# Loading one chunk of q later in a sliding-window attention and gated feed-forward kernel

## The chip, the cores and the metric

The kernel runs on one core of a Trainium2 chip. The metric is the device time of one execution in microseconds (us); the time of a version is the median of several executions. A profiled execution of the version before is used for everything that is said of its inside.

The engines of a core work side by side: PE multiplies matrices, DVE and ACT do elementwise work, POOL does elementwise work and also issues loads, SP issues stores and transposes. Sixteen DMA engines move the data; the loads that POOL issues go through one queue (q0 in the profile), SP's transfers through another (q1).

## The reference

Eight batches with eight heads, 576 tokens and 64 elements per head. Each token attends to itself and the 63 tokens before it; the result goes through a feed-forward layer with the gate h * cos(h).

```python
scores = scale * np.matmul(q, k.transpose(0, 1, 3, 2))      # q, k, v: (8, 8, 576, 64)
rel = pos[:, None] - pos[None, :]
mask = (rel >= 0) & (rel < 64)
scores = np.where(mask, scores, -1000000000.0)
attn = softmax(scores)
x = np.matmul(attn, v)                                      # to (4608, 512)
h = x @ w_in                                                # w_in: (512, 2048)
out = (h * np.cos(h)) @ w_out                               # w_out: (2048, 512)
```

## The kernel before

The 4608 tokens are cut into nine tiles of 512. For each tile `mt` from 1 on, PE runs through the same stage: 64 matmuls for `h_ps` (L512), with the sine on ACT (L748) and the gate on DVE (L751), and then 64 for `out_ps` (L764; from tile 6 on a form with fewer products, L601). Between them, attention work for later tiles is put in: in tile `mt` the scores of batch `mt + 1` (L327, two bursts: the first after the `h_ps` matmuls, the second after 24 of the `out_ps` matmuls), then mask and row maximum on DVE (L380), exponentials on ACT (L392), reciprocals on DVE (L402), normalised weights `w` on POOL (L409), and their transposition to `wT` by DMA from SP (L428). At the end of tile `mt` PE forms the value products of tile `mt + 1` (L444: 64 small matmuls of `wT` and `v`), copies take them to `xT`, and the next tile's `h_ps` starts from there. So the value products stand between two stages, and they need the last `wT` that the tile made. A tile's weights come in five groups (tile 2) or four (tiles 3 to 5) before this point, and more after it, whose `wT` are read one tile later.

q and k of a batch from 2 on are loaded in five chunks of up to 128 tokens, all heads at once: four chunks of 128 rows and a fifth of 64 (`load_chunk`, issued by POOL at L186, with the conversion to bf16). They are turned by DMA transposes that SP issues (`turn`, L243), three for q into `qT` and three for k into `kT`: chunks 0 and 1, chunks 2 and 3, chunk 4 (`TURNS`, L45). v is loaded in five chunks as well (L192), and POOL copies halves of it to shifted places (`spread_v`, L130).

What stands where is set by a plan: `at(time, function, arguments)` (L615) puts a step at a planned time, and `pump` (L618) emits all steps up to a time, in the order of their times. A tile is 32 units of this plan. Each engine then works through its own instructions in that order, and an instruction that waits for data holds up everything behind it on its engine. Planned times are an order only; the chip doesn't know them. The loop at L648 plans the loads of the batches from 2 on. For batch 4, `t0` is 96 and the loads fall into tile 2 (times 64 and on): its q chunks are at 5.6 + 1.6 c behind 64 (L655), of its k chunks the first two in between, and chunks 2 to 4 at 24.2 + 0.01 c (L657). `spread_v` of batch 3 is at 24.0 and 24.1 in the same count (L670), the three turns of q of batch 4 at 24.3, 24.32 and 24.34 (L651), the turns of k six units ahead of tile 3 and in the order of L662.

Of the kernel before, what the change touches and what calls it, by code (L numbers as in the profile page):

```python
# [43 lines left out]
NB = 5  # L44
# [30 lines left out]
def kernel(  # L75
# [539 lines left out]
    def at(time, fn, *args):  # L615
        plan.append((time, len(plan), fn, args))
# [8 lines left out]
    for i, (b, jobs, banks) in enumerate(bursts):  # L625
        t = T * (b - 1)
        at(t + (BURST[i % 2] + 0.9 * (i == 1) if b < B - 1 else (17.2, T + 14.6)[i % 2]), burst_scores, i)
        for n in range(jobs[0][0], jobs[-1][-1] + 1):
            place = (n - n_listed) % NU
            time = t + BURST[0] + PACE * place  # L630
# [17 lines left out]
    for b in range(2, B):  # L648
        t0 = T * (b - 1)
        for lo, hi in TURNS:  # L650
            at(t0 - (2.01 - 0.1 * lo if b == 2 else T - (24.3 if b == 4 else 23.4) - 0.01 * lo), turn_q, b, lo, hi)  # L651
        if b > 2:
            for c in range(NB):
                for i, name in enumerate(("q", "k")):
                    time = 17.9 + 2.8 * i if b == 3 and c == NB - 1 else 5.6 + 1.6 * c + 0.8 * i  # L655
                    if name == "k" and (b == 3 or c > (1 if b == 4 else 2)):
                        time = ((24.31 if c > 1 else 13) if b == 3 else 24.2 if b == 4 else 22.4) + 0.01 * c  # L657
                    if b > 4 and c == 0:
                        time = (24.26 if b == 5 else 22.46) + 0.01 * i - T
                    at(t0 - T + time, load_chunk, name, b, c)  # L660
        for lo, hi in TURNS:
            at(t0 + 0.1 * lo - (2 if b == 2 else 6), turn_k, b, lo, hi)  # L662
        for c in range(5):
            at(t0 + (10.1 + 0.1 * c if b == B - 1 else 0.5 + c), load_v, b, c)
        for half_ in range(2):
            if b == 2:
                at(t0 + 24.1 + 0.01 * half_, spread_v, b, half_, "p", 0, 2)
                at(t0 + 24.2 + 0.1 * half_, spread_v, b, half_, "p", 2, 4)
            else:
                at(t0 + (24 if b == 3 else 27.5 if b == B - 1 else 22.2) + 0.1 * half_, spread_v, b, half_)  # L670
    for mt in range(2, n_mt):
        for p in range(PAIRS):
            time = T * mt - 1.01
# [130 lines left out]
```

## Time and profile before

| what | value |
| --- | --- |
| three runs | 296.73, 297.04, 298.02 us; median 297.04 |
| the profiled execution | 296.9 us |
| its span, from the first to the last instruction | 295.1 us |
| granted TensorE clock | 1.000 |
| stage of tile 2 in the trace | 87.3 to 118.4 us |
| stage of tile 3 in the trace | 118.4 to 148.8 us |
| q0, the queue of POOL's loads | 100896 packets, 18.06 MB |
| q1, SP's queue | 67184 packets, 25.15 MB |

The page gives each engine's busy time over the span, the chain of work that ended last, and groups of instructions. Times in its rows are us from the span's start. A group that ends with a bracket was idle before it, and the bracket names what ended that. A DMA row gives the KB and the us from issue to landing.

### The profile page before, as it was taken

What the parts mean: (1) busy time and instruction counts of PE and PEld (TensorE: products, weight loads), DVE (VectorE), ACT (ScalarE), POOL (GpSimd) and SP (SyncE); (2) the same over time, 40 slices, a digit from 0 to 9 for tenths busy, and PEclk for the clock granted to TensorE, in tenths of its full rate; (3) what the DMA queues carried; (4) which work ended last, traced back from release to release, by engine and by line L of the source; (5) the groups of instructions that cost most, each with busy time, mean ns of one, the idle gap of its engine ahead of it and who ended that gap; (6) DMA issues with size and microseconds to landing.
All of it is one profiled execution on the core that took longest, in us unless ns stands there. A gap on an engine that the chain in (4) does not pass through costs nothing.

```text
span 295.1 us, 8290 instructions
## 1 busy us (share of the span) xinstructions
PE 287.7 (97%) x2815; PEld 162.7 (55%) x2815; DVE 230.6 (78%) x906; ACT 238.1 (81%) x791; POOL 210.0 (71%) x230
## 2 busy tenths in 40 slices
PE   8979999999999999999999999999999999999995
PEld 3658854544454444444454545444547854884595
DVE  4988888887897876788678876996689878957853
ACT  5998699888987799879987999799977896937710
POOL 9899659992899659994999399948995476133200
PEclk9999999999999999999999999999999999999999
DMA  7999999999999999999999999999959415042013
GB/s 139 180 199 205 192 193 146 150 136 149 186 214 137 144 227 153 143 178 216 171 171 144 220 168 161 147 211 187 144 121 192 53 38 178 2 116 84 0 38 107
DMA packets 168267, 43.81 MB, mean 148 GB/s; under 512 B 155616, under 2 KB 163872, under 8 KB 168224
## 3 DMA queue, kind: packets, MB, share of 16 engines
q0 software_dynamic: 100896, 18.06, 84.0%
q1 hardware_dynamic: 67184, 25.15, 48.0%
q8 instruction: 22, 0.36, 0.5%
q14 instruction: 21, 0.17, 0.2%
q10 hardware_dynamic: 144, 0.07, 0.1%
HBM read 36.70 MB, written 9.44 MB: 156 GB/s over the span
## 4 chain that ended last, share of the span: by engine, by line
PE 85%; POOL 6%; DMA 3%; ACT 3%; DVE 1%; issue 1%; POOLq 0%
PE h_ps L512 37%; PE out_ps L764 19%; PE out_ps L601 13%; PE h_ps L476 5%; PE o_ps L444 3%; PE out_ps L495 3%; ACT e L392 2%; PE s_ps L327 2%; POOL w L409 2%; DMA k<-in_k_dram 2%; DMA wT<-w 1%; POOL v L192 1%; PE tw_ps L425 1%; POOL w_in L208 1%; POOL v L130 1%
## 5 line engine op out<-in xcount | busy, mean ns | idle before, releaser
L512 PE MATMUL h_ps<-xT,w_in 128*128 128x512 bf16 x512 | 111.8, 379 | 0.0
L409 POOL TENSOR_TENSOR w<-e,rden 128x512 bf16<-128x512 f32 (+1 forms) x68 | 69.5, 1033 | 47.9 <-DVE rden L402 36.7
L751 DVE TENSOR_TENSOR gT<-h_ps,sin 128x512 bf16<-128x512 f32 x128 | 84.6, 687 | 21.8 <-ACT sin L748 20.4
L392 ACT ACTIVATE e<-s,negm 128x128 f32<-128x128 f32 (+1 forms) x256 | 97.2, 382 | 2.6 <-DVE negm L380 1.6
L748 ACT ACTIVATE sin<-h_ps 128x512 f32<-128x512 f32 x128 | 73.6, 599 | 25.4 <-PE h_ps L512 23.5
L512 PEld LDWEIGHTS <-w_in 128*128 128x128 bf16 x512 | 50.0, 98 | 59.5
L764 PE MATMUL out_ps<-w_out,gT 128*128 128x512 bf16 x320 | 72.0, 380 | 0.0
L380 DVE CUSTOM_DVE_ANT_0 s<-s_ps,mask 128x128 f32<-128x128 f32 (+1 forms) x256 | 55.8, 277 | 0.3 <-PE s_ps L327 0.3
L764 PEld LDWEIGHTS <-gT 128*128 128x128 bf16 x320 | 30.4, 98 | 35.4
L392 ACT ACTIVATION_READ_ACCUMULATOR e<-s,negm 128x1 f32 x256 | 48.1, 188 | 0.0
L192 POOL DMA_DIRECT2D v<-in_v_dram x40 | 34.0, 874 | 0.4 <-issue 0.3
L186 POOL DMA_DIRECT2D q<-in_q_dram x30 | 26.3, 888 | 4.0 <-PE tq_ps L225 2.8
L186 POOL DMA_DIRECT2D k<-in_k_dram x30 | 26.2, 884 | 0.0
L402 DVE RECIPROCAL rden<-den 128x4 f32<-128x4 f32 (+1 forms) x73 | 12.0, 167 | 17.8 <-ACT e L392 17.6
L130 POOL COPY v<-v 64x1536 bf16<-64x1536 bf16 (+3 forms) x16 | 22.9, 1431 | 0.4
L380 DVE DVE_READ_ACCUMULATOR2_ANT negm<- 128x1 f32 x256 | 21.3, 83 | 0.0
L541 POOL TENSOR_TENSOR qT<-gT 128x512 bf16<-128x512 bf16 x12 | 13.6, 1151 | 9.1 <-DVE gT L751 9.0
L130 DVE CAST xT<-o_ps 128x512 bf16<-128x512 f32 x24 | 15.5, 681 | 5.7 <-PE o_ps L444 5.5
L601 PEld LDWEIGHTS <-gT 128*128 128x128 bf16 x152 | 14.0, 98 | 2.2
L495 PE MATMUL out_ps<-w_out,gT 128*128 128x512 bf16 x64 | 14.7, 380 | 0.0
L476 PE MATMUL h_ps<-xT,w_in 128*128 128x256 bf16 x128 | 14.6, 273 | 0.0
L572 DVE TENSOR_TENSOR out_sb<-out_ps,p 128x512 f32<-128x512 f32 (+2 forms) x16 | 8.6, 549 | 6.7 <-ACT p L130 5.6
(92 smaller groups left out, 326.0 us busy)
## 6 DMA issues: line engine op xcount, KB each, us to landing
out_dram<-out_sb SPq DMA_DIRECT2D x16, 512.0 KB, 8.8
v<-in_v_dram POOLq DMA_DIRECT2D x32, 128.0 KB, 6.0
q<-in_q_dram POOLq DMA_DIRECT2D x24, 128.0 KB, 9.0
k<-in_k_dram POOLq DMA_DIRECT2D x24, 128.0 KB, 6.7
w_in<-in_moe_w_in_dram POOLq DMA_DIRECT2D x4, 512.0 KB, 9.3
w_out<-in_moe_w_out_dram POOLq DMA_DIRECT2D x4, 512.0 KB, 10.7
q<-in_q_dram POOLq DMA_DIRECT2D x7, 144.0 KB, 5.8
k<-in_k_dram POOLq DMA_DIRECT2D x7, 144.0 KB, 5.9
```

What stands on the lines that cost most here:

```text
L130: {"a": nc.scalar.copy, "p": nc.gpsimd.tensor_copy}.get(engine, nc.vector.tensor_copy)(out, in_)
L186: nc.gpsimd.dma_start(out=st[name, b][0:n, c].rearrange("p (h d) -> p h d", h=H), in_=src.rearrange("h p d -> p h d"))
L192: nc.gpsimd.dma_start(out=vt.rearrange("p (h d) -> p h d", h=H), in_=v[b, :, c * 128:c * 128 + n, :].rearrange("h p d -> p h d"))
L380: nc.vector.tensor_tensor_reduce(out=s[:, u, c], in0=s_ps[:, u, c], in1=mask[:, 2 - j % 2 if j else 0, c], scale=-scale if b else -1.0, sc ...
L392: nc.scalar.activation(e[:, u, c], s[:, u, c], AF.Exp, bias=negm[:, u:u + 1], scale=1.0 if n < n_first else -1.0, accum_out=den[:, u:u + 1])
L409: (nc.gpsimd if engine == "p" else nc.vector).tensor_tensor(out=w[:, 0:u], in0=e[:, 0:u], op=ALU.mult, in1=rden[:, 0:u].unsqueeze(2).to_br ...
L476: nc.tensor.matmul(out=h_ps[:, half * e:half * e + half], lhsT=w_in_sb[:, ks, ff * 128:ff * 128 + 128], rhs=st["xT", 0][:, ks, half * g:ha ...
L512: nc.tensor.matmul(out=st["h", ff], lhsT=w_in_sb[:, ks, ff * 128:ff * 128 + 128], rhs=st["xT", mt][:, ks], start=start, stop=stop)
L601: nc.tensor.matmul(out=to[n_] if split else to[:, e], lhsT=lhs[name][f // 2][:, f % 2, 128 * e:128 * e + 128], rhs=rhs[name][:, f, lo:hi], ...
L748: nc.scalar.activation(sin, h_ps, AF.Sin, bias=math.pi / 2.0)
L751: nc.vector.tensor_tensor(out=gt[:, e], in0=h_ps, in1=sin, op=ALU.mult)
L764: nc.tensor.matmul(out=o_ps[e], lhsT=gT[ff // 2][:, ff % 2, ms * 128:ms * 128 + 128], rhs=w_out_sb[:, ff], start=ff == 0, stop=ff == n_ff - 1)
```

## The change

Of batch 4, the load of q's fifth chunk (64 rows) is planned at 24.19 instead of 12.0, in the count in which k's chunks 2 to 4 stand at 24.22 to 24.24. No other step's time is changed.

```diff
@@ -655,6 +655,8 @@
                     time = 17.9 + 2.8 * i if b == 3 and c == NB - 1 else 5.6 + 1.6 * c + 0.8 * i
                     if name == "k" and (b == 3 or c > (1 if b == 4 else 2)):
                         time = ((24.31 if c > 1 else 13) if b == 3 else 24.2 if b == 4 else 22.4) + 0.01 * c
+                    if name == "q" and b == 4 and c == NB - 1:
+                        time = 24.19
                     if b > 4 and c == 0:
                         time = (24.26 if b == 5 else 22.46) + 0.01 * i - T
                     at(t0 - T + time, load_chunk, name, b, c)
```

On POOL, in the middle of tile 2, the load moves behind five weight products (`w`) and two copies of v, to the place ahead of k's chunks 2 to 4. The names in brackets are the counters that an instruction waits for: DMASW those of POOL's own earlier loads, DMAHW those of SP's transfers, DVE and Pool those of the engines.

```order
 L186 DMA q<-in_q_dram 128x8x64 [waits DMASW2_49]
 L186 DMA q<-in_q_dram 128x8x64 [waits DMASW3_49]
-L186 DMA q<-in_q_dram 64x8x64 [waits DMASW4_49]
 L409 TENSOR_TENSOR w<-e,rden 128x512 [waits DMAHW6_49,DVE_49]
 L409 TENSOR_TENSOR w<-e,rden 128x512 [waits DMAHW7_49,DVE_49]
 L409 TENSOR_TENSOR w<-e,rden 128x512 [waits DMAHW0_49,DVE_49]
 L409 TENSOR_TENSOR w<-e,rden 128x512 [waits DVE_49] x2
-L130 COPY v_78<-v_78 64x3x512
+L130 COPY v_78<-v_78 64x3x512 [waits DMASW4_49]
 L130 COPY v_78<-v_78 64x4x512 [waits Pool_49]
+L186 DMA q<-in_q_dram 64x8x64
 L186 DMA k<-in_k_dram 128x8x64 [waits DMASW5_49]
```

Only the 64-row load moved; the wait for an earlier load (DMASW4, one of v's) that it had carried is now carried by the first copy. As no other load stands between the two places, the loads follow each other in the same order as before.

On SP no row moved. At the end of tile 2 stand there, in both kernels, the last transpose of w that tile 3's value products read, the three turns of q, one more transpose of w and the three turns of k:

```order
L428 DMA_TRANSPOSE wT<-w 128x4x128 [waits DMAHW0_49,Pool_49]
L243 DMA_TRANSPOSE qT_75<-q 128x8x128 [waits DMASW6_49,DMAHW1_49,DMASW0_49,PE_49]
L243 DMA_TRANSPOSE qT_75<-q 128x8x128 [waits DMASW3_49,DMAHW2_49,DMASW2_49,PE_49]
L243 DMA_TRANSPOSE qT_75<-q 128x4x64 [waits DMAHW3_49,DMASW4_49,PE_49]
L428 DMA_TRANSPOSE wT<-w 128x4x128 [waits DMAHW4_49,Pool_49]
L243 DMA_TRANSPOSE kT<-k 128x8x128 [waits DMAHW5_49,DMASW7_49,DMASW1_49]
L243 DMA_TRANSPOSE kT<-k 128x8x128 [waits DMAHW6_49,DMASW6_49,DMASW5_49]
L243 DMA_TRANSPOSE kT<-k 128x4x64 [waits DMAHW7_49,DMASW7_49]
```

The third turn of q (64 columns wide) is the one that waits for the moved load (its DMASW4); in the program it stood behind the load by five weight products and two copies of POOL, and now nothing of POOL's stands between the two.

## The prediction

> **What bounds the kernel now.** I read the head of the page first, then the chain that ended last in order of time, then the busy time by stage.
>
> ```profile
> span 295.1 us, 8290 instructions
> PE 287.7 (97%) x2815; PEld 162.7 (55%) x2815; DVE 230.6 (78%) x906; ACT 238.1 (81%) x791; POOL 210.0 (71%) x230
> ```
>
> PE is busy for 287.7 of 295.1 us. A change in loads can only win what PE waits, and the whole kernel holds 7.4 us of that, the start and the end included. So the question is small: does PE wait anywhere for something that the moved load delays, and does the move make it wait elsewhere? I call the moved load (q, batch 4, fifth chunk, 64 rows) the tail. The next rows are the chain where it leaves PE near the tail, and the stage of tile 2 beside that of tile 3 (columns: stage, its length, busy us of PE, PEld, DVE, ACT, POOL with counts, clock, DMA share, GB/s).
>
> ```profile
> 111.01 1.04 POOL w L409
> 112.05 0.55 POOL v L130
> 112.60 4.42 DMA wT<-w
> 87.30:118.40 31.10, 30.77 (x265) 14.67 (x264) 23.15 (x109) 27.20 (x95) 25.06 (x27) 1.00 1.74 164
> 118.40:148.80 30.40, 30.40 (x265) 14.49 (x264) 23.23 (x109) 27.19 (x95) 25.73 (x28) 1.00 1.91 177
> ```
>
> With the same 265 matmuls tile 2 takes 31.10 us and tile 3 takes 30.40: 0.70 us more. The chain says where: the last normalised weights (w, POOL, 111.01 to 112.05) go through one DMA transpose, issued at 112.60 and landed 4.42 us later, at 117.02. PE's timeline shows who reads it (start, us, what, idle before); the last row is the view of PE's waits from 56 to 240 us, which holds no other (us in total, times, longest).
>
> ```profile
> 116.15 0.62 PE L444 MATMUL o_ps<-wT,v 128*64 128x64 bf16 x14
> 117.07 0.98 PE L444 MATMUL o_ps<-wT,v 128*64 128x64 bf16 x50 [0.30 <-DMA wT<-w]
> 147.24 1.20 PE L444 MATMUL o_ps<-wT,v 128*64 128x64 bf16 x64
> ...
> PE o_ps L444 <- DMA wT<-w: 0.3, 1, 0.3
> ```
>
> The 64 value products of a tile take 1.20 us undisturbed (tile 3). Here 14 start at 116.15, the fifteenth needs that last transpose, and the 64 end at 117.07 + 0.98 = 118.05: 1.90 us. So 1.90 - 1.20 = **0.70 us is all that PE loses here**, the same as the difference of the stages (the view of waits counts only the 0.3 between the two groups, since a matmul's modelled end lies later than the start of the next).
>
> **The change, step by step.** One instruction moves on POOL. These are POOL's rows around its old and its new place.
>
> ```profile
> 101.21 0.69 POOL L186 DMA_DIRECT2D q<-in_q_dram  x1 [0.95 <-DMA kT<-k]
> 104.97 1.03 POOL L409 TENSOR_TENSOR w<-e,rden 128x512 bf16<-128x512 f32 x1 [3.07 <-DVE rden L402]
> 112.00 3.41 POOL L130 COPY v<-v 64x1536 bf16<-64x1536 bf16 x2
> 115.35 2.50 POOL L186 DMA_DIRECT2D k<-in_k_dram  x3
> 119.66 4.03 POOL L409 TENSOR_TENSOR w<-e,rden 128x512 bf16<-128x512 f32 x4
> 131.31 1.65 POOL L186 DMA_DIRECT2D q<-in_q_dram  x2
> 136.06 1.03 POOL L409 TENSOR_TENSOR w<-e,rden 128x512 bf16<-128x512 f32 x1 [3.10 <-DVE rden L402]
> ```
>
> 1. At the old place POOL gets 0.69 us back, and the 0.95 us that it waited there. Worth nothing: its next work waits 3.07 us for DVE anyway.
>
> 2. At the new place, 115.35, everything behind on POOL starts 0.69 us later: three k chunks, two first chunks of batch 5, four w, v's loads, batch 5's chunks. The last of these would end at 131.31 + 1.65 + 0.69 = 133.65, and at 136.06 POOL waits 3.10 us for DVE: the delay is gone there. The four w are read by tile 4 at 147 and cover it.
>
> 3. The gain: the tail's packets leave the software queue (q0), which shares the 16 DMA engines with the transposes (q1). Landings first (the last figure is us from issue): the tail, tile 2's last transpose of w, tile 5's (with its issue at 202.48), and a lone one after 240 us. Then the packets, MB and share of q0 from 112 to 114, 114 to 116 and 120 to 122 us.
>
> ```profile
> q<-in_q_dram POOLq DMA_DIRECT2D x1, 64.0 KB, 13.7
> wT<-w SPq DMA_TRANSPOSE x1, 4.4
> 202.48 1.19 SPq L428 DMA_TRANSPOSE wT<-w  x1
> wT<-w SPq DMA_TRANSPOSE x1, 3.6
> wT<-w SPq DMA_TRANSPOSE x1, 2.4
> q0 software_dynamic: 414, 0.05, 40.0%
> q0 software_dynamic: 21, 0.00, 2.0%
> q0 software_dynamic: 1489, 0.19, 354.7%
> ```
>
> The tail landed at 101.21 + 13.7 = 114.9, so it was in the engines during the last transposes of w. Its 64 KB are 512 packets of 128 B (0.19 MB in 1489 packets is 128 B each). When q0 had most of the engines it moved 1489 packets in 2 us; 512 packets are then 0.69 us of all engines. How much of that the last transpose sees is not in the trace. **Lower end 0**: from 114 to 116 q0 moved only 21 packets, so most of its backlog had left before the transpose (4.4 us) had much in flight, and a lone transpose takes 2.4 us of the 4.4 whatever is taken away. **Upper end 0.70**, all that PE waits: q0's last packets still came after 114, just when the tail landed, and the slowest engine sets the landing; the last transpose of tile 5's w took 3.6, 0.8 us less than this one. Could it come later instead? In this stretch only work is taken out, so I exclude it. I take **0.5 us**, nearer to the 0.69 of engine time than to zero, because the landing 114.9 lies inside this transpose's flight of 112.6 to 117.0.
>
> 4. The new wait: SP turns q in three transposes, and the third reads the tail. SP works in order, so what stands behind waits too: one transpose of w, the three of k, three of w, two stores. SP's rows, then the landings of the three k transposes, then the first k load at 115.35 and the last, then the two places at which PE reads k and q of batch 4.
>
> ```profile
> 117.16 1.46 SPq L243 DMA_TRANSPOSE qT<-q  x1
> 120.72 1.51 SPq L428 DMA_TRANSPOSE wT<-w  x1
> 122.33 1.25 SPq L243 DMA_TRANSPOSE kT<-k  x1
> 126.19 1.20 SPq L243 DMA_TRANSPOSE kT<-k  x1
> kT<-k SPq DMA_TRANSPOSE x1, 4.4
> kT<-k SPq DMA_TRANSPOSE x1, 6.5
> k<-in_k_dram POOLq DMA_DIRECT2D x1, 128.0 KB, 5.0
> k<-in_k_dram POOLq DMA_DIRECT2D x1, 64.0 KB, 6.9
> 132.12 0.59 PE L327 MATMUL s_ps<-kT,qT 64*64 64x64 bf16 x32
> 137.92 0.86 PE L327 MATMUL s_ps<-kT,qT 64*64 64x128 bf16 x40
> ```
>
> A load issued at 115.35 behind the same copies landed in 5.0 us with twice the bytes, so I put the tail at 115.35 + 5.0 = 120.35. The third turn of q starts there instead of at 117.16, 3.2 us later, and ends at 121.81; the transpose of w (its w ready at 119.66 + 1.03 + 0.69 = 121.38) then runs to some 123.4, and k's first turn starts near 123.5 instead of 122.33: **1.2 us late**, because 2.1 us of the hold fall into time in which SP was waiting for POOL's w. It lands at 123.5 + 4.4 = 127.9; PE wants it at 132.12. Cover left: 4.2 us. k's last turn waits for the last k load (now some 1.4 us later at most: 0.69 for its issue, as much for the tail's packets), starts near 127.6 and lands at 134.1, and PE reads it only late in the burst at 137.92: 3.8 us left. Cost **0** for PE, while that cover lasts.
>
> 5. Given back in tile 3: batch 5's loads are 0.69 us later against the transposes of w there, and PE comes 0.5 us sooner. The row of the last such transpose and its landing:
>
> ```profile
> 141.63 1.19 SPq L428 DMA_TRANSPOSE wT<-w  x1
> wT<-w SPq DMA_TRANSPOSE x1, 4.8
> ```
>
> It landed at 141.63 + 4.8 = 146.43, 0.81 us ahead of PE's products at 147.24. If the whole shift of 0.69 + 0.5 = 1.19 us came through, PE would wait 0.38 us; if w's transposes simply follow PE, nothing. I take nothing, since the w there follow DVE (3.10 us of wait at 136.06), which follows PE; 0.4 stays as the upper end.
>
> The sum: 0 (POOL) - 0.5 (stall of tile 2) + 0 (SP's hold) + 0 (tile 3) = -0.5 us. The profiled execution took 296.9 us, with a span of 295.1; 296.9 - 0.5 = 296.4. The median of the runs before, 297.04, lies 0.14 above the profiled execution, so by the median it would be 296.5, which I predict.
>
> A rule bears on step 3. The Trainium skill, "DMA: Bandwidth & Descriptors", section "Queues, rings and completion order", says that each DMA engine takes turns between the queues it has work for, a packet at a time. By that rule every packet of the tail taken away gives the transposes its turn, and the gain would be the full stall; the row with 21 packets of q0 speaks against so much. That is the third rival below.
>
> **Rivals.**
>
> *No gain (chance 0.28).* The last transpose is slow by its own issue and completion, not by the tail. For: 2.4 us of 4.4 stay in any case, and q0 had 21 packets left after 114. Against: the tail's landing at 114.9. Or the gain is won and given back in tile 3. Then 296.9, up to 297.3 with step 5's 0.4.
>
> *SP held too long (0.07): slower.* These rows are the medians of the 64 KB loads of q and of k.
>
> ```profile
> q<-in_q_dram POOLq DMA_DIRECT2D x6, 64.0 KB, 12.6
> k<-in_k_dram POOLq DMA_DIRECT2D x6, 64.0 KB, 5.8
> ```
>
> If the tail still took its 13.7 us, it would land at 129.05; the turn ends at 130.5, the transpose of w at 132.1, k's first turn lands at 132.2 + 4.4 = 136.6, and PE, which wants it at 132.12, stands still for 4.5 us: 301.4. It decides from a landing of 9.2 us on (k's first turn must start by 127.72; 1.46 + 1.51 and two gaps of 0.1 before it). For: q's median of 12.6. Against: those loads stood last behind the others; k's, issued where the tail now goes, take 5.8. The Trainium skill speaks for still less: the same page, section "Anatomy of one DMA", fits a DMA from GpSimd by about 2.0 us and its bytes over 436 GB/s, an estimate of 2.15 us for 64 KB and hardly a hold; no load of this size in the rows above comes near it, so the rows decide.
>
> *The whole stall goes (0.10).* Every engine is freed by the tail's packets just before the last transpose, which lands 0.7 us sooner, as tile 5's 3.6 shows to be possible: 296.9 - 0.7 = 296.2.
>
> That the change does nothing is excluded: the order of POOL shows the load moved.
>
> **How the numbers follow.** Forecast 0.55 (296.4 to 296.5), no gain 0.28, whole stall 0.10, SP held 0.07. A difference of 0.5% (1.5 us), about what a measurement of this kernel can tell from no change, is more than twice the largest gain, so faster has 0.02, for a PE wait that this profile hides. Slower takes the SP rival's 0.07, less the part of it below 1.5 us: 0.06. Same: 0.92. The range: from 296.2 less the 0.3 by which the lowest run before (296.73) lies below its median, to 297.3 plus 0.5 for a run between the median and the highest (298.02): 295.9 to 297.8.
>
> **What would show it.** Right: the last transpose of w in tile 2 lands in about 3.9 us instead of 4.4, and the 64 value products take 1.2 to 1.5 us instead of 1.90; the third turn of q starts near 120.3 on SP, k's first turn near 123.5, and no PE wait appears at the score bursts near 132 and 138. Wrong: the stall of tile 2 unchanged (rival one), a PE wait for kT near 132 (rival two), a new wait at tile 3's value products near 147 (step 5). The prediction fails as a whole if the tail takes over 9 us to land.

## The result, and the profile after

| version | median | all executions | ratio to before, 95% |
| --- | --- | --- | --- |
| before | 297.02 us | 20, 295.94 to 298.76 | |
| changed | 300.74 us | 20, 296.94 to 301.61 | 1.0077 (1.0054 to 1.0100) |

The change makes the kernel slower, by 0.8%, and it makes it scatter. Eight of the twenty executions took 296.94 to 299.44 us at a mean granted clock of 0.999 or 1.000; the other twelve took 299.81 to 301.61 us, ten of them at 0.987 to 0.994. Ratios leave out executions over 1.5% above the kernel's shortest. The profiled execution is one of the short ones: 297.44 us, with a span of 295.7.

The head of its page shows nothing. PE's busy time is the 287.7 us of before, in a span 0.6 us longer.

```profile
span 295.7 us, 8290 instructions
PE 287.7 (97%) x2815; PEld 162.7 (55%) x2815; DVE 230.7 (78%) x906; ACT 238.2 (81%) x791; POOL 209.9 (71%) x230
```

PE's timeline at the value products shows what happened (start, us, what, idle before it and what ended that). The first row ends tile 2, the next three tile 3, the fifth tile 4. The last row is the view of PE's waits.

```profile
116.21 1.20 PE L444 MATMUL o_ps<-wT,v 128*64 128x64 bf16 x64
146.60 0.38 PE L444 MATMUL o_ps<-wT,v 128*64 128x64 bf16 x12
147.44 0.19 PE L444 MATMUL o_ps<-wT,v 128*64 128x64 bf16 x1 [0.46 <-DMA wT<-w]
148.03 0.98 PE L444 MATMUL o_ps<-wT,v 128*64 128x64 bf16 x51 [0.41 <-DMA wT<-w]
178.21 1.20 PE L444 MATMUL o_ps<-wT,v 128*64 128x64 bf16 x64
PE o_ps L444 <- DMA wT<-w: 0.9, 2, 0.5
```

At the end of tile 2 the 64 products take 1.20 us: the whole stall of 0.70 is gone. At the end of tile 3, where before had none, they run from 146.60 to 148.03 + 0.98 = 149.01, 2.41 us instead of 1.20: **1.21 us lost**. With the 296.9 us of before's profiled execution, 296.9 - 0.70 + 1.21 = 297.4, which is what this one took. So its account closes; why the median lies 3.3 us higher is taken up below.

The places at which the prediction looked for harm are unharmed. The rows: the tail on POOL and its landing, SP's third turn of q, the transpose of w behind it, the first turn of k and its landing.

```profile
115.41 0.73 POOL L186 DMA_DIRECT2D q<-in_q_dram  x1
q<-in_q_dram POOLq DMA_DIRECT2D x1, 64.0 KB, 5.5
120.96 1.17 SPq L243 DMA_TRANSPOSE qT<-q  x1
122.23 1.21 SPq L428 DMA_TRANSPOSE wT<-w  x1
123.55 1.25 SPq L243 DMA_TRANSPOSE kT<-k  x1
kT<-k SPq DMA_TRANSPOSE x1, 4.0
```

The tail landed at 115.41 + 5.5 = 120.9, and k's first turn went out at 123.55 (predicted 123.5) and landed at 127.6; no wait shows at the score bursts.

The new wait is at a transpose that the change doesn't touch. The chain of work that ended last, around tile 3's value products, and then the last two transposes of w there on SP's queue with the landing of the last (us from issue):

```profile
139.93 1.04 POOL w L409
140.97 0.29 POOL v L130
141.25 6.74 DMA wT<-w
148.03 0.98 PE o_ps L444 x51
...
141.25 2.47 SPq L428 DMA_TRANSPOSE wT<-w  x1
wT<-w SPq DMA_TRANSPOSE x1, 6.7
```

It was issued 0.38 us sooner than before (141.25 instead of 141.63) and landed 1.6 us later (147.99 instead of 146.43), because it was 6.7 us on its way instead of 4.8. The bytes that moved just before it show why. The view of stretches, first before, then changed (stretch, its length, busy us of PE, PEld, DVE, ACT, POOL, clock, DMA share, and last GB/s):

```profile
137.00:138.00 1.00, 1.00 (x9) 0.34 (x11) 1.00 (x9) 1.00 (x7) 0.38 (x2) 1.00 1.51 265
138.00:139.00 1.00, 1.00 (x42) 0.79 (x43) 0.69 (x8) 1.00 (x6) 0.76 (x1) 1.00 1.22 322
139.00:140.00 1.00, 1.00 (x6) 0.44 (x5) 0.82 (x8) 1.00 (x7) 0.98 (x1) 1.00 1.24 327
```

```profile
137.00:138.00 1.00, 1.00 (x42) 0.70 (x40) 0.81 (x8) 1.00 (x6) 0.92 (x1) 1.00 2.54 38
138.00:139.00 1.00, 1.00 (x11) 0.45 (x6) 0.87 (x8) 1.00 (x7) 0.73 (x2) 1.00 0.96 132
139.00:140.00 1.00, 1.00 (x6) 0.44 (x5) 0.51 (x4) 1.00 (x7) 0.50 (x2) 1.00 1.26 328
```

The 320 GB/s are tile 2's two stores of 512 KB (L521). In the changed kernel the engines moved 38 GB/s for a microsecond while work was queued: a **standstill** (28 packets of 256 B or less, begun from 137.04 on, took about 1.0 to 1.4 us each, the typical one taking 0.03). The stores then ran from 138.56 to 142.83 (from the packet records) instead of 137.09 to 141.97, into the time of the last transpose.

### The profile page after: what moved, and what is told of

Read it like the earlier page. It is cut to its first block, busy times and chain, and to the rows that moved or that the text cites. A ratio compares the mean times of both kernels' runs of the same rounds, so it can differ in the third digit from the quotient of the medians.

```text
span 295.7 us, 8290 instructions
## 1 busy us (share of the span) xinstructions
PE 287.7 (97%) x2815; PEld 162.7 (55%) x2815; DVE 230.7 (78%) x906; ACT 238.2 (81%) x791; POOL 209.9 (71%) x230
## 4 chain that ended last, share of the span: by engine, by line
PE 85%; POOL 5%; DMA 4%; ACT 2%; DVE 1%; issue 1%; POOLq 0%
PE h_ps L512 37%; PE out_ps L766 19%; PE out_ps L601 13%; PE h_ps L476 5%; PE o_ps L444 3%; PE out_ps L495 3%; DMA wT<-w 2%; PE s_ps L327 2%; POOL w L409 2%; ACT e L392 2%; DMA q<-in_q_dram 2%; POOL v L192 1%; PE tw_ps L425 1%; POOL w_in L208 1%; POOL v L130 1%
```

## The experiments

The theories changed on the way, and the expectations name them. At the start there were two. *Collision*, later called the *loads theory*: batch 5's loads come 0.7 us later and PE 0.7 us sooner, so the last transposes of w in tile 3 land behind those loads. *SP's hold*: the third turn of q waits for the moved load and delays what stands behind it on SP. The *stores theory* came after the first runs: tile 2's two stores stand late in SP's queue, in front of tile 3's transposes of w. Last came the *sum theory*: the three shifts that the change makes (PE sooner at tile 3, batch 5's loads later, SP's work around the third turn later) together use up the 0.81 us of slack in front of tile 3's value products. Its rivals: two of the shifts are enough (*pair theory*), the wait of the third turn for its load is itself needed, or the scatter has nothing to do with the change.

### The changed kernel again

The kernel as it is, on two other occasions.

> The changed kernel as it is, to see its spread and, with luck, a profile of one of its long executions (over 300 us; 11 of 20 before). Both theories expect a median near 300.7 against 297.0 before. Collision (batch 5's loads come 0.7 us later and PE 0.7 us sooner, so that the last transposes of w in tile 3 land behind those loads): a PE wait of 1 to 4 us at tile 3's value products, and none in tile 2. SP's hold (the third turn of q waits for the moved load and delays k's turns and the stores): waits at the score bursts of tile 3, or k's first turn landing after 132. If a long execution shows a granted clock below 1.0 behind a PE wait of over 1 us, the rest of the loss is the clock's.

> The changed kernel once more, beside the fourth cell on the same chip. Theory of the sum: the same as the fourth cell within 1 us, 298.5 to 300.5. Rival (the turn's own wait is needed): 1 us or more above the fourth cell.

| run | median | lowest to highest | ratio, 95% |
| --- | --- | --- | --- |
| late_again | 299.03 | 297.07 to 303.60 | 1.0052 (1.0015 to 1.0088) |
| after_third | 299.18 | 296.28 to 302.62 | 1.0028 (0.9991 to 1.0064) |

Of its 44 executions on the three occasions 20 took 300 us or more; of the 154 executions of the kernel before, over all occasions, four did. The loss comes back, but its size varies from occasion to occasion. The profile of late_again caught a long execution, 301.87 us; it shows only how a long one looks. PE's timeline at tile 3, then the stage behind it:

```profile
147.91 0.38 PE L444 MATMUL o_ps<-wT,v 128*64 128x64 bf16 x12
148.96 0.19 PE L444 MATMUL o_ps<-wT,v 128*64 128x64 bf16 x1 [0.68 <-DMA wT<-w]
150.88 1.28 PE L444 MATMUL o_ps<-wT,v 128*64 128x64 bf16 x51 [1.73 <-DMA wT<-w]
152.49 15.09 PE L512 MATMUL h_ps<-xT,w_in 128*128 128x512 bf16 x64
148.80:179.20 30.40, 28.51 (x237) 13.62 (x237) 20.46 (x88) 22.95 (x73) 20.67 (x23) 0.94 1.72 178
```

The same wait, longer: 152.16 - 147.91 - 1.20 = 3.05 us lost. Behind it the granted clock of the stage is 0.94, and the 64 matmuls take 15.09 us instead of 13.98 as in the other profiles: 1.1 us more. The Trainium skill, "TensorE: Matmul & The Clock Gate", section "HAM oscillation — how this bites in real kernels", has the clock fall once PE is idle for more than some 3.4 us; here idle stretches of 0.68 and 1.73 us with 0.19 us of work between were followed by it, so, if they brought it on, the measured bound is lower than the page's. This execution has another lowered stretch in its first 25 us (14.8 to 18.2 us), ahead of the change's place: after_third's profile has one too (19.4 to 22.8 us), and so have three kernels of the next sections, one of them the kernel before with other stores. The profile of after_third, at 298.06 us, has 0.49 us lost at tile 3.

### One part at a time

The three shifts apart. spare_load: the kernel before, plus a load of the tail's rows into rows of the buffer that nothing reads, at the place to which the change moved it.

```diff
+    def load_spare():
+        nc.gpsimd.dma_start(out=st["q", 4][64:128, NB - 1].rearrange("p (h d) -> p h d", h=H),
+                            in_=q[4, :, 512:576].rearrange("h p d -> p h d"))
...
+                    if name == "q" and b == 4 and c == NB - 1:
+                        at(t0 - T + 24.19, load_spare)
```

> The kernel before, with one load more: the same 64 rows of q of batch 4 are loaded a second time at the changed place, into rows of the tile that nothing reads. POOL is as late as in the changed kernel and the queue as full, but q's third turn waits for nothing new, and tile 2 keeps its stall, so PE comes no sooner. Collision: half of its cause is there (loads 0.7 us later), so 297.0 to 299.5 with a part of the executions long. SP's hold: 297.0, no long executions.

turn_only: the kernel before, with the third turn of q behind k's turns.

```diff
-            at(t0 - (2.01 - 0.1 * lo if b == 2 else T - (24.3 if b == 4 else 23.4) - 0.01 * lo), turn_q, b, lo, hi)
+            at(t0 - 5.5 if b == 4 and lo == 4 else t0 - (2.01 - 0.1 * lo if b == 2 else T - (24.3 if b == 4 else 23.4) - 0.01 * lo), turn_q, b, lo, hi)
```

> The kernel before (moved load at its old place), with the third turn of q of batch 4 behind the three turns of k. Nothing is loaded later; only SP is busier where it had been idle less, so its two stores of tile 2's output start about 1.2 us later (133.2 instead of 132.0). Stores theory (the loss comes from those stores, 1 MB, standing late in SP's queue in front of tile 3's transposes of w): tile 3's value products start to wait, 0.3 to 1.2 us, and the time is 297.3 to 298.5. Loads theory (batch 5's loads 0.7 us later against a PE that is 0.7 us sooner): no wait in tile 3, 297.0.

tail_tile1: the tail loaded a tile sooner, behind k of batch 3, so that its packets are gone from the end of tile 2 and nothing else changes there.

```diff
+                    if name == "q" and b == 4 and c == NB - 1:
+                        time = 24.5 - T
```

> The chunk loaded one tile earlier, behind the loads of k of batch 3 in tile 1: it is out of tile 2's loads as in the changed kernel, but SP's turn has nothing to wait for, and no load of tile 2's end or tile 3 is late. Both theories: tile 2's wait shrinks, tile 3 has none, 296.3 to 296.9. If tile 3 still waits over 1 us and the time is over 298, PE's earlier arrival alone is enough for the loss and both theories fall.

The pairs, each the two edits above together: spare_turn (load and turn), tile1_turn (tail and turn), tile1_spare (tail and load).

> The kernel before, with the unread second load of the chunk at the changed place and the third turn of q behind k's turns: POOL and SP are as late as in the changed kernel with the turn behind k, but nothing waits for the moved load. Stores theory: the stores start 1.2 us late, the standstill comes in part of the executions, median 297.5 to 299 with a part over 300. If the wait for the moved load itself were needed: 297.0, none over 300.

> The chunk loaded in tile 1 (so PE comes sooner at the end of tile 2) and the third turn of q behind k's turns (so SP is later), no load late. Sum theory (each of the three latenesses uses up a part of one slack of 0.8 us in tile 3): 297.2 to 298.2, some executions over 299. Pair theory (only late loads together with late SP cost): 296.6.

> The chunk loaded in tile 1, and the unread second load of it at the changed place: PE sooner and the loads behind it 0.7 us later, SP as before. Sum theory: 297.2 to 298.2. Pair theory: 296.6.

All three: turn_after_k is the changed kernel with turn_only's edit (its third turn waits for nothing); tile1_spare_turn is the three edits above in the kernel before, so that no turn waits for a late load.

> The changed kernel, with the third turn of q of batch 4 behind the three turns of k, so that SP is not held by the moved load. Collision: nothing gained, a median of 300 to 301 with long executions as in the changed kernel. SP's hold: the loss goes, 296.3 to 297.0.

> The fourth cell: batch 4's fifth q chunk is loaded in tile 1 (so its packets are gone from the end of tile 2 and PE is sooner), an unread load of the same size stands where the change put the chunk (so batch 5's loads are later), and the third turn of q stands behind k's turns (so SP's work around it is later), while no turn waits for a load at that place. Theory of the sum of the three shifts: each alone cost nothing, pairs cost 0 to 0.8 us over the kernel before, and all three together use up the 0.81 us of slack at tile 3's value products: a median of 298 to 299, some executions over 300, and in the profile a wait at tile 3's or tile 4's value products for the transposes of w. Rival, the wait of the third turn for its load is itself needed: no more than the pairs, under 297.9, and no such wait.

two_tails doubles the change: batch 5's fifth q chunk is late as well (`b in (4, 5)`, at 22.39 for batch 5).

> The changed kernel, with the fifth chunk of q of batch 5 moved in the same way, in front of k's late chunks in tile 3. Takes 64 KB out of the loads that collide with tile 3's transposes of w. Collision: the wait in tile 3 goes, 296.3 to 297.5, unless the same happens one tile later (then 298 to 301, with the PE wait in tile 4). SP's hold: not mended, and a second hold in tile 3: 300.7 or more.

| run | median | ratio, 95% | lost at tile 3 in its profile, us |
| --- | --- | --- | --- |
| spare_load | 297.06 | 1.0004 (0.9975 to 1.0034) | 0 |
| turn_only | 297.39 | 0.9994 (0.9966 to 1.0021) | 0 |
| tail_tile1 | 296.65 | 0.9992 (0.9961 to 1.0023) | 0 |
| spare_turn | 297.86 | 1.0025 (1.0000 to 1.0051) | 0 |
| tile1_turn | 297.24 | 1.0004 (0.9969 to 1.0040) | 0 |
| tile1_spare | 297.60 | 1.0013 (0.9983 to 1.0042) | 0 |
| turn_after_k | 298.39 | 1.0040 (1.0017 to 1.0064) | 1.4 (and 0.34 at tile 4) |
| tile1_spare_turn | 298.12 | 1.0020 (0.9992 to 1.0048) | 1.26 |
| two_tails | 300.94 | 1.0041 (1.0002 to 1.0080) | 2.34 (and 0.56 at tile 4) |

(two_tails' ratio rests on six of its 12 executions, so its median says more. One execution of spare_load took 595 us and one of its before 494 us; neither is in a ratio.) No shift costs anything alone that can be told, no pair costs over 0.25% or shows the wait, and with all three the wait is back, without the late load's wait too: all five profiles with the three shifts have it (0.49 to 3.05 us), none of the seven with fewer. Collision alone is out by spare_load, whose profile has the late loads and almost no stall in tile 2; SP's hold alone is out by turn_after_k, for which it had 296.3 to 297.0 us; and two_tails, where collision had the wait of tile 3 gone, kept it. This is tile1_spare_turn at tile 3, and tail_tile1 at the ends of tiles 2 and 3:

```profile
147.05 0.46 PE L448 MATMUL o_ps<-wT,v 128*64 128x64 bf16 x12
148.18 0.19 PE L448 MATMUL o_ps<-wT,v 128*64 128x64 bf16 x1 [0.67 <-DMA wT<-w]
148.53 0.98 PE L448 MATMUL o_ps<-wT,v 128*64 128x64 bf16 x51 [0.16 <-DMA wT<-w]
```

```profile
116.37 1.20 PE L444 MATMUL o_ps<-wT,v 128*64 128x64 bf16 x64
146.76 1.20 PE L444 MATMUL o_ps<-wT,v 128*64 128x64 bf16 x64
```

tail_tile1 wins the 0.70 us of tile 2 and loses nothing at tile 3, and its median lies 0.3 us below its before (296.99), too little to be told from no change. The stall of tile 2 is not as firm as one profile made it look: of the six profiles with the tail at its old place four have 0.6 to 0.75 us of it and two (spare_load, turn_only) at most 0.1; of the fourteen with the tail elsewhere one has as much (tile1_spare, 0.64), so in that profile PE isn't sooner, and it is spare_load's that stands for that pair. The sum of the shifts holds for the wait. It doesn't explain all of the median: tile1_spare_turn and turn_after_k, whose third turn waits for no load, had one execution each of 12 at 300 us or more, the changed kernel 20 of 44. The runs after_third and tile1_spare_turn, side by side on the same chip, have 299.18 and 298.12: 1.06 us apart, just what the rival had asked for, with intervals that overlap. So the third turn's own wait may add to the long executions; that stays open, and no profile shows how. turn_only, whose profile shows no wait, had two executions of ten above 302 us as well; its ratio rests on the other eight.

### What the stores do

no_store: the changed kernel without tile 2's two stores.

```diff
-                at(base + T + 0.5 + ms0 / 2, store, o_sb, mt, ms0, 0, 2)
+                if mt != 2:
+                    at(base + T + 0.5 + ms0 / 2, store, o_sb, mt, ms0, 0, 2)
```

> The changed kernel without the two stores of tile 2's output, 512 rows of the result, which are left out. Stores theory: no standstill, no wait in tile 3, 296.0 to 296.8. Loads theory: q0 keeps its loads at the same place, so the wait in tile 3 stays over 0.5 us.

The median is 296.55 us, its ratio 0.9982 (0.9959 to 1.0005), and none of its ten executions is above 297.57. No value product waits, though the DMA engines stand still all the same (PE at tile 3, then the stretches as above):

```profile
147.11 1.20 PE L444 MATMUL o_ps<-wT,v 128*64 128x64 bf16 x64
```

```profile
137.00:138.00 1.00, 1.00 (x20) 0.40 (x22) 1.00 (x9) 1.00 (x6) 0.41 (x1) 1.00 2.47 100
138.00:139.00 1.00, 0.84 (x41) 0.71 (x31) 0.68 (x8) 1.00 (x7) 0.73 (x2) 1.00 0.93 56
139.00:140.00 1.00, 1.00 (x6) 0.49 (x5) 0.69 (x8) 1.00 (x6) 0.94 (x1) 1.00 2.40 157
```

So the stores don't make the standstill, and without them the value products lose nothing by it. The forecast of the stores theory came for the time and the wait, not for the standstill, which it had expected to go. Six kernels tried to put the stores elsewhere.

store_late: the changed kernel with tile 2's second store behind tile 3's transposes of w. store_early: its first store in front of the third turn of q.

```diff
-                at(base + T + 0.5 + ms0 / 2, store, o_sb, mt, ms0, 0, 2)
+                at(base + T + (23.35 if mt == 2 and ms0 else 0.5 + ms0 / 2), store, o_sb, mt, ms0, 0, 2)
```

```diff
-                at(base + T + 0.5 + ms0 / 2, store, o_sb, mt, ms0, 0, 2)
+                at(base + (24.33 if mt == 2 and not ms0 else T + 0.5 + ms0 / 2), store, o_sb, mt, ms0, 0, 2)
```

> The changed kernel, with the second of tile 2's two stores (512 KB) behind the four transposes of w of tile 3. Stores theory: half of what stands ahead of them is gone (512 KB at the 300 GB/s that the stores reach, 1.7 us), tile 3's wait of 1.2 to 2.6 us falls to 0 to 0.9, 296.3 to 297.3, no long executions. Loads theory: the wait stays, 298 to 301.

> The changed kernel, with the first of tile 2's two stores in front of the third turn of q, where SP stands waiting for the moved load anyway. Stores theory: as with the store moved behind, 296.3 to 297.3, no long executions, and SP's later work no later than in the changed kernel. Loads theory: 298 to 301.

stores_ahead (changed kernel) and stores_ahead_old (kernel before): both stores ahead of the last three transposes of w of tile 2.

```diff
-                at(time + lags[4], g_trans, n)
+                at(T * b + 1.6 + 0.01 * place if b == 3 and place > 5 else time + lags[4], g_trans, n)
```

> The changed kernel, with the two stores of tile 2's output in front of the last three transposes of w that tile 2 issues (read only one tile later), so that they start moving some 5 us sooner. Stores theory in its second form (what decides is whether the stores' data has begun to move when tile 3's first transpose of w is issued; where it has not, the queues stand still for 1 to 1.5 us, and the stores' 3.5 us follow): no standstill, tile 3's wait 0 to 0.3, median 296.2 to 297.0 and no execution over 300. Loads theory (tile 3's transposes are late because batch 5's loads are): wait and long executions stay, 298.5 to 301.

> The kernel before with the same change of the stores alone. Both theories: it has no wait in tile 3 to lose, so 296.5 to 297.3, tile 2's wait of up to 0.7 us unchanged. If it is as fast as the changed kernel with the stores ahead, the moved load itself brings nothing.

act_stores (changed) and act_stores_old (before): the two stores issued by ACT, on a queue of their own.

```diff
-        nc.sync.dma_start(out=out[r0:r0 + n * 128].rearrange("(a p) f -> p a f", p=128), in_=o_sb[:, e:e + n])
+        (nc.scalar if mt == 2 else nc.sync).dma_start(out=out[r0:r0 + n * 128].rearrange("(a p) f -> p a f", p=128), in_=o_sb[:, e:e + n])
```

> The changed kernel, with tile 2's two stores issued by ACT between the sines of tile 3 instead of by SP. If the stores cost by standing ahead of tile 3's transposes in SP's queue: the transposes share the engines with the stores instead of waiting behind them, the wait in tile 3 shrinks below 0.5 us, 296.3 to 297.3, none over 300. If they cost by their use of the DMA engines: 298.5 to 301 as before.

> The kernel before, with the same two stores issued by ACT. It waits for nothing in tile 3, so both theories give 296.7 to 297.2; ACT's two issues lie beside PE's h_ps matmuls.

| run | median | ratio, 95% | what its profile shows |
| --- | --- | --- | --- |
| store_late | 301.82 (4 runs) | none | 0.5 us lost at tile 3, 3.6 at tile 4 |
| store_early | 299.40 | 1.0062 (1.0035 to 1.0090) | 0.7 at tile 3, 1.6 at tile 4 |
| stores_ahead | 301.76 | 1.0125 (1.0076 to 1.0175) | 4.7 at tile 3 |
| stores_ahead_old | 298.60 | 1.0044 (1.0021 to 1.0066) | 1.5 at tile 3 |
| act_stores | 301.84 | 1.0134 (1.0084 to 1.0184) | ACT waits 4.75 (below) |
| act_stores_old | 301.72 | 1.0144 (1.0103 to 1.0184) | ACT waits 4.06 (below) |

None helps, and no forecast of the stores theory came for any of the six; stores_ahead_old missed both theories, and only store_early's 299.40 us is what the loads theory had. store_late and store_early, with one of the two stores behind the standstill instead of both, lose 0.5 and 0.7 us at tile 3, and moved part of the loss to the next tile. stores_ahead was a surprise: the stores' data were through by 137.66 (changed) and 136.55 (before), long ahead of the last transpose, and it got worse. There a standstill and a loss stand without stores behind it, but the edit also put three transposes of w between the stores and tile 3's; what of the 4.7 us is theirs wasn't measured. The last pair tells nothing of the stores. In ACT's timeline of act_stores the store that ACT issues stands behind a turn of q, and the sine behind the store:

```profile
125.80 0.43 ACTq L521 DMA_DIRECT2D out_dram<-out_sb  x1
126.28 0.60 ACT L750 ACTIVATE sin<-h_ps 128x512 f32<-128x512 f32 x1 [4.75 <-DMA qT<-q]
```

ACT does nothing for 4.75 us, and PE loses 3.4 us waiting for the gate behind it (view of waits). The edit put a new wait of its own into the stage (the store waits for the counter that its own landing counts up, one that SP's transfers use as well), so the time is not that of stores on another queue.

### What the standstill stands behind

The packet records of all these profiles were read around it. In the changed kernel, a slice of 0.1 us ahead of the standstill has one packet of the instruction queue (q8) beside transposes and loads; before has its like at 137.0. The last line of the second group is before's whole microsecond from 137, the third group the changed kernel's. (The first row of each counts the packets by size; the queue's row has its packets, their MB and their time as a share of the slice.)

```profile
DMA packets 79, 0.03 MB, mean 312 GB/s; under 512 B 78, under 2 KB 78, under 8 KB 78
q8 instruction: 1, 0.02, 80.4%
```

```profile
DMA packets 97, 0.03 MB, mean 329 GB/s; under 512 B 95, under 2 KB 95, under 8 KB 96
q8 instruction: 1, 0.02, 68.2%
...
DMA packets 522, 0.27 MB, mean 265 GB/s; under 512 B 427, under 2 KB 427, under 8 KB 521
```

```profile
DMA packets 202, 0.04 MB, mean 38 GB/s; under 512 B 202, under 2 KB 202, under 8 KB 202
```

Before: 521 - 427 = 94 packets of at least 2 KB, the stores' data. Changed: none. The table sets side by side the time at which SP issued the first of tile 2's stores and, from the packet records, the 16 KB instruction packet, the first 2 KB packet of those stores, and the standstill (packets of up to 2 KB that took over 0.5 us).

| kernel | first store issued | instruction packet | first data of the stores | standstill | lost at tile 3 |
| --- | --- | --- | --- | --- | --- |
| before | 131.99 | 137.02 | 137.09 | none | 0 |
| turn_only | 131.50 | 136.31 | 136.64 | none | 0 |
| tile1_turn | 131.94 | 137.01 | 136.66 | none | 0 |
| spare_turn | 133.09 | 138.05 | 138.03 | none | 0 |
| tile1_spare | 132.56 | 138.54 | 137.72 | none | 0 |
| tail_tile1 | 130.65 | 136.70 | 135.57 | none | 0 |
| spare_load | 131.76 | 138.16 | 136.47 | none | 0 |
| changed | 132.33 | 136.37 | 138.56 | 137.04 to 138.53 | 1.21 |
| tile1_spare_turn | 133.08 | 136.79 | 139.20 | 137.48 to 138.85 | 1.26 |
| turn_after_k | 133.53 | 137.35 | 139.56 | 137.87 to 139.41 | 1.4 |
| two_tails | 133.79 | 137.72 | 139.95 | 138.36 to 139.75 | 2.34 |
| late_again | 133.78 | 137.49 | 139.93 | 138.19 to 139.68 | 3.05 |
| after_third | 132.88 | 137.62 | 137.95 | 138.16 to 139.75 | 0.49 |
| no_store | none | 136.67 | none | 137.55 to 138.75 | 0 |

Where the stores' data had begun before the instruction packet or up to 0.33 us behind it there was no standstill, save in after_third, at 0.33, where the loss is the smallest and only 15 of the stores' own packets took that long. Where the packet fell among transposes and loads alone, the engines stood still from 0.5 to 0.9 us later on, for 1.2 to 1.6 us, and the stores came out of it into the last transpose.

The first data can't come while the engines stand still, so their time is in part the standstill's own effect. The issue of the store isn't, as it lies 3.7 us or more ahead of the packet, and it parts the kernels too: SP issued the first store 4.8 to 6.4 us ahead of the packet where nothing is lost, 4.74 us in after_third, and 3.7 to 4.0 us where 1.2 us or more is lost. The packet goes with PE: it stands 9.2 to 10.4 us ahead of PE's value products in every kernel of the table. So before, with 5.03 us, is 1 us from the changed kernel's 4.04, and this is how the 1 us goes: PE, and with it the packet, comes 0.65 us sooner, and the store goes out 0.34 us later.

The 16 KB instruction packets between 70 and 185 us in 18 of the profiles (all but act_stores and act_stores_old) say the same: of 37 with at least ten of the stores' packets around them (0.5 us before to 0.6 behind), one was followed within 1.6 us by ten or more packets of 256 B or less that took over 0.9 us; of 84 with fewer of those and at least 150 packets of transposes (256 B), 69 were. Counted the other way, over all 20 profiles, 84 of 91 such groups of slow packets in that stretch begin within 2 us behind a 16 KB packet. The one exception of the 37 is stores_ahead, where the stores' data had just ended. That fits what it and stores_ahead_old showed: early stores leave the packet among transposes alone.

This was read off after the runs, and no run moved an instruction packet by itself: that the packet is the cause is **argued, not shown**. What is shown is that in the kernels of the table the loss comes where the standstill has the stores' data in or behind it, that without the stores it is gone (no_store), and that before is 1 us from it.

## Why the prediction was wrong

*What bounds the kernel* was right: PE waited at one place for one transpose. *Step 1* (nothing from POOL's old place) and *step 2* (0.7 us later behind the new place, gone by the next weight) held: at the next weight POOL still waits for DVE (first row; the second is the landing of tile 2's last transpose of w).

```profile
135.42 1.03 POOL L409 TENSOR_TENSOR w<-e,rden 128x512 bf16<-128x512 f32 x1 [1.71 <-DVE rden L402]
wT<-w SPq DMA_TRANSPOSE x1, 3.9
```

*Step 3*, the gain, was under-sized: 0.5 was taken and the upper end of 0.70 came, which the text had as the third rival. That transpose landed in 3.9 us, as foretold. The rule of the Trainium skill on turns by packet, "DMA: Bandwidth & Descriptors", section "Queues, rings and completion order", by which the full stall would go, stood on the right side in this profile; tail_tile1, where the tail is out of the way too, gets the same 0.70. But the stall isn't in each profile with the tail at its old place: over the six it is 0.47 us in the mean, over the fourteen others 0.09. So the gain is nearer to 0.4 than to 0.70, as far as profiles of different kernels tell, and that 0.5 lies near it is luck: the prediction took it from another reason.

*Step 4*, the hold of SP, was right to 0.6 us at each row (tail 120.9 for 120.35, third turn 120.96, k's first turn 123.55 for 123.5), and it cost PE nothing at the score bursts. The rival built on it fell. But the step asked only what k's turns lose, and not what SP's shift does to the stores behind them.

***Step 5* is the one that failed.** It set 0.81 us of slack against a shift of 1.19, gave 0.4 as the upper end and took 0, "since the w there follow DVE, which follows PE". That reason was right: the last transpose went out 0.38 us sooner, with PE 0.64 sooner. The slack was even some 0.2 us more than 0.81, as 13 products go ahead of the one that reads this transpose. Left out was that its landing isn't a constant. It took 4.8 us with the stores' data coming from 137.09 on, and 6.7 with a standstill and the data from 138.56 on. The stores stand in step 4's list of what SP's hold delays, but neither step gave them a price. Measured at this term: 1.21 us in the profiled execution (0.49 and 3.05 in the other two profiles of this kernel), where 0 to 0.4 stood. By the profiled execution the sum would then be -0.70 + 1.21 = +0.5, inside the range: the first rival's "won and given back in tile 3", at three times the price that it had.

*The range and the chances* failed on a second count. One execution stood for all, as before's agree within 1%. The changed kernel's don't: in three profiles its wait is 0.49, 1.21 and 3.05 us, and behind the longest the clock falls for another 1.1. No execution of it between 300 and 301.6 us was profiled, so how the median of 300.74 comes about is argued: late_again's 301.87 us hold 1.3 that were lost before the places of the change (the value products that end tile 1 begin at 87.12, in the first profile of the changed kernel at 85.82), part of them in the lowered stretch near 16 us, and without them it is 300.6, beside the seven executions of 300.71 to 300.99. A lowered clock alone doesn't do it: tail_tile1 has executions at 0.987 and 0.992 that took 298.32 and 296.63 us. The chance for slower, 0.06, had the wrong place: on k's turn in front of PE instead of on the stores a tile further on.

No version beats the kernel before by more than can be told: tail_tile1, the best that computes all, is at 0.9992 (0.9961 to 1.0023).

## What to carry to other kernels

A transfer's time from issue to landing in a profile is not a property of that transfer: before setting it against a slack, look at what else is in the DMA engines while it flies, and whether the change moves that, even where no instruction there changes. A slack of under 1 us in front of the busiest engine should be priced with a landing as slow as the worst of its kind in the profile, and shifts that are each free should be tried together. Where a change makes executions scatter, one profile has the mechanism but not the price.

## What the hardware showed that was not expected

- The DMA engines can all but stand still for 1.2 to 1.6 us with work queued (38 GB/s in one microsecond, 328 two later), mostly within 1 us behind a 16 KB packet of the instruction queue among DMA transposes: 69 of 84 such packets, against 1 of 37 with the stores' 2 KB packets around it. The Trainium skill, "Runtime: NRT & Kernel Launch", section "Instruction fetch mechanics", has instructions refilled in blocks of 16 KiB over the sequencer's own DMA queue, at a cost that is mostly hidden. The blocks of 16 KB show here; if the packet is the cause, the transposes beside it paid for it.
- An idle time of 0.68 and 1.73 us of PE, 0.19 us of work between, was followed by a stage at a granted clock of 0.94; 0.65 and 1.35 us in two_tails were not (1.00). Over the profiles the clock fell behind losses of 3.05, 3.64 and 4.70 us at the value products (late_again, store_late, stores_ahead), and behind none of 2.34 us or less.
- A store that ACT issues waited for a turn of q from SP's queue, 4.75 us, and the sine behind it with it. The wait is the program's (a counter that both use), not one of the queues.
